# Attention and two gated layers on one core: other planner durations, six planning passes, shorter masks, and a choice of engine for divisions and copies

## Chip, core and metric

One core of one Trainium2 chip runs the whole program. The time is the device time of one execution in microseconds (us); of the kernel before there are three timed runs and one profiled execution. Engine names as in the profile: PE is TensorE, with PEld its weight loads; DVE is VectorE; ACT is ScalarE; POOL is GpSimd; SP is SyncE, which issues nearly all DMAs.

## What is computed

Three stages follow each other; all inputs and outputs are float32 and the weights are given as 64-bit floats (the kernel rebuilds float32 from their two halves).

```python
# 1. attention: 2 batches, 8 heads, 768 positions, head width 64
keep = (pos_k < n_global) | ((rel >= 0) & (rel < n_local))       # 8 and 96
scores = q @ k.T / 8 - slope[h] * dist, -1e9 where not keep
x = softmax(scores) @ v                                          # to (2, 768, 512)
# 2. first gated layer, causal convolution over 5 positions
x = (sigmoid(conv5(x)) * (x @ w_val)) @ w_out
# 3. second gated layer, centred convolution over 3 positions, width 1024
h = relu(x @ w_in)
out = (h * sigmoid(conv3(h))) @ w_out2
```

## The kernel before

**Attention.** Since a query sees the first 32 positions at most and a short band behind itself, there are 12 tiles (2 batches of 6) of 128 queries against at most 256 keys. For each tile and half (4 heads): scores on PE into PSUM (L430); on DVE the masked score and its minimum, by one custom instruction per head that reads the scores from PSUM and the mask `B` from SBUF (L441, "the minimum" below); on ACT the exponential with its sum (L446); on POOL the guard of four sums (L457); on DVE the reciprocal (L460) and one division of the 128x256 (first tile of a batch: 128x128) probabilities per head (L467). PE turns the probabilities, two heads at a time, into PSUM (L491), ACT copies them out (`pts`, L495), PE multiplies by the values (L509), and ACT copies the tile's output into `x` (L526).

**Weights.** A weight of 512 KB is loaded into `raw`, and ACT (L238), POOL (L240) and DVE (twice, L245 and L248) make it float32. There are three `raw` buffers and 24 such loads. The first layer's output weight and the second's input weight are multiplied on PE beforehand (L295, product `W`).

**Gated layers.** They run over four chunks (two per batch, 400 and 368 positions). Matmuls take three products of split halves: a high part made on ACT (L210) and a low part on DVE (L212). `values` makes `gg` from `gx` (L674), `hidden` makes `h` from `gg` and `W` (L715), `gated` makes `g` (L734), `project` the output (PE into bank `s`, copied by L769 and L771). A convolution is one scaled copy for its first tap (L616 on ACT, or L617 on POOL) and DVE multiply-adds for the others (L621).

**What sets the order.** Every step is added to a `Plan` with an engine, an assumed duration and what it reads and writes. `Plan.lay` runs a list schedule backward for ranks and once forward; the order of starts is then the program's order on PE, DVE, ACT and POOL, and within one engine nothing overtakes. Steps with several "ways" go to the engine where the schedule ends them first. Buffers are rings: a step that opens a buffer waits for the users of the one it replaces. Masks are prepared before the plan by hand: distances and their comparisons on DVE, one scaled copy of the mask per head on POOL (L335).

Of the kernel before, what the change touches and what calls it, by code (L numbers as in the profile page):

```python
# [81 lines left out]
class Plan:  # L82
# [31 lines left out]

    def link(self):
# [13 lines left out]
    def lay(self, pred, succ, rank, back):  # L129
# [3 lines left out]
        free = dict.fromkeys(self.LAG, 0.0)  # L133
        mode, est, at = None, dict.fromkeys(self.work, 0.0), {}
# [41 lines left out]
    def issue(self, laid):  # L176
        self.link()
        order = list(self.work)
        if laid:
            back = self.lay(lambda w: w.succ, lambda w: w.pred, lambda w: 0.0, True)  # L180
            for w in self.work:
                w.rank = -back[w] - w.cost + w.bias
            at = self.lay(lambda w: w.pred, lambda w: w.succ, lambda w: w.rank, False)
            order.sort(key=lambda w: at[w])
# [43 lines left out]
def to_f32(c, dst, raw, n, bufs, reads, token):  # L228
# [9 lines left out]
    pl.add("ACT", act_us(n), lambda: nc.scalar.activation(dst(), whole(), AF.Copy, scale=2.0**-112), bufs, reads, [token])  # L238
# [11 lines left out]
    pl.add("DVE", dve_us(n, 0.12), last_bits, bufs, [], [tail])  # L250
    pl.add("DVE", dve_us(n, 0.12), join, bufs, [tail], [token])


def conv_weights(c):
# [3 lines left out]
    c.plan.add("SP", 0.5, lambda: nc.sync.dma_start(raw.rearrange("p d t -> p (d t)"), c.conv_w), writes=["cwr"], delay=2.5)  # L258
# [5 lines left out]
def unit(c, dst, src, a, col, bufs, token, e=None):  # L264
# [3 lines left out]
    c.plan.add("SP", 0.5, dma, [raw], [], [("raw", raw)], delay=4.0)  # L268
# [4 lines left out]
def weights(c):  # L273
# [14 lines left out]
    def product(half):  # L288
        wi = "inb" if half else "ina"
        for cb in range(4):  # L290
            ps = c.ring["f"].new()
            cs, fs = slice(cb * P, (cb + 1) * P), slice(half * 512, (half + 1) * 512)
            for e in range(4):
# [7 lines left out]
                512, [ps], [("wps", half, cb)], ("W", half, cb),  # L301
# [24 lines left out]
def scratch(c):  # L326

    x = [c.x[:, d, XP:] for d in range(NC1)]
    c.rel, c.ge, c.loc, c.d = (x[d][:, 0:WIN] for d in range(4))
    c.key, c.k0, c.d0, ic = (x[d][:, 4 * P : 5 * P] for d in range(4))  # L330
    return c.d.bitcast(I32), ic.bitcast(I32)


def mask_head(c, out, d, h):
    c.nc.gpsimd.tensor_scalar(out, d, -slope(h) / QKSCALE, 1.0, ALU.mult, ALU.mult)  # L335


def first_mask(c):
# [5 lines left out]
    rel, loc, key, k0, d0 = c.rel, c.loc, c.key, c.k0, c.d0  # L344
# [5 lines left out]
    c.b0 = c.const.tile([P, 2, P], F32, name="b0")  # L350
    c.B0 = [c.b0[:, h, :] for h in range(2)]
    for h in range(2):
        mask_head(c, c.B0[h], d0, h)


def masks(c, ap):

    nc, pl = c.nc, c.plan
    ng, nl, rel, loc, d, key = c.ng, c.nl, c.rel, c.loc, c.d, c.key
    c.B = ap.tile([P, NH, WIN], F32, name="B")  # L360
    b0 = ap.tile([P, NH - 2, P], F32, name="b02")
    c.B0 += [b0[:, h, :] for h in range(NH - 2)]
    for h in range(2, NH):
        pl.add("POOL", 0.33, lambda h=h: mask_head(c, c.B0[h], c.d0, h), [], ["d0"], [("B0", h)])

    def distance():
        nc.vector.tensor_scalar(key[:, 0:GW], key[:, 0:GW], ng, None, ALU.is_lt)
        nc.vector.tensor_scalar(d, loc, -BIG, BIG, ALU.mult, ALU.add)
        nc.vector.tensor_scalar(d[:, 0:GW], key[:, 0:GW], -BIG, BIG, ALU.mult, ALU.add)
        nc.vector.tensor_tensor(d[:, GW:], d[:, GW:], rel[:, GW:], ALU.add)  # L370
        nc.vector.tensor_scalar(d[:, 0:GW], d[:, 0:GW], nl, None, ALU.add)
# [583 lines left out]
```

## Time and profile before

| what | us |
|---|---|
| timed runs | 297.34, 297.78 (median), 299.58 |
| profiled execution, its own time | 296.97 |
| its span | 295.2 |
| outside the span | 1.8 |

The span is what the profile shows, and the execution's own time adds 1.8 us around it. Busy time is the time in which an engine works on at least one instruction; on DVE, ACT and PE the end of one record overlaps the start of the next, so the distance from start to start is a little less than a record's length.

### The profile page before, as it was taken

The page shows a single profiled execution, that of the slowest core. Times are in us where ns is not written, and L with a number is a line of the kernel's source. Part 1 is how long each engine was busy: PE and PEld are TensorE (multiplying, and loading weights), DVE is VectorE, ACT ScalarE, POOL GpSimd, SP SyncE. Part 2 cuts the span into 40 slices and gives each one's busy share as a digit, 9 for nine tenths or more (in the row PEclk, how much of TensorE's full clock was granted, in tenths as well). Part 3 has the DMA queues.
Part 4 walks back from the last instruction along what each step waited for, and adds up shares of the span by engine and source line. Part 5 has one row for each costly group of instructions (what it writes and reads, how often), then busy time and mean ns, then how long its engine had stood idle before and what let it go on. Part 6 is the DMA issues. An engine that isn't in the chain of part 4 may idle for free.

```text
span 295.2 us, 5444 instructions
## 1 busy us (share of the span) xinstructions
PE 271.7 (92%) x1832; PEld 227.5 (77%) x1832; DVE 238.3 (81%) x638; ACT 198.8 (67%) x498; POOL 57.4 (19%) x153
## 2 busy tenths in 40 slices
PE   2398897999998999999999999999999999999990
PEld 2366775664554699999898899989999988999890
DVE  4789998899999999999799999999996643367500
ACT  2589999998386879798689663895466523466410
POOL 2831112234211210032212440011220200000000
PEclk9999999999999999999999999999999999999998
DMA  4953478564514521002412000000000000000111
GB/s 139 361 221 112 149 255 273 180 194 163 165 52 142 154 107 38 19 2 95 151 49 71 2 1 36 3 0 36 36 2 37 36 2 36 36 2 3 71 73 44
DMA packets 10277, 26.18 MB, mean 89 GB/s; under 512 B 1408, under 2 KB 2688, under 8 KB 10240
## 3 DMA queue, kind: packets, MB, share of 16 engines
q1 hardware_dynamic: 9440, 25.22, 25.1%
q10 hardware_dynamic: 800, 0.52, 0.6%
q8 instruction: 16, 0.26, 0.4%
q14 instruction: 21, 0.17, 0.2%
HBM read 22.59 MB, written 3.15 MB: 87 GB/s over the span
## 4 chain that ended last, share of the span: by engine, by line
PE 75%; DMA 8%; ACT 5%; issue 4%; DVE 3%; SPq 2%; POOL 1%; POOLq 0%; DVEq 0%; ACTq 0%
PE f L295 8%; PE f L219 8%; PE s L220 7%; PE s L221 7%; PE s L219 7%; PE f L221 7%; PE f L220 7%; PE x L509 4%; PE t L491 3%; PE s L430 3%; ACT p L446 3%; DMA v<-in_v_dram 3%; PE x L221 2%; PE t L221 2%; PE x L219 2%
## 5 line engine op out<-in xcount | busy, mean ns | idle before, releaser
L446 ACT ACTIVATE p<-p,st 128x256 f32<-128x256 f32 (+1 forms) x96 | 46.0, 483 | 7.8 <-DVE st L441 7.7
L621 DVE SCALAR_TENSOR_TENSOR z<-h,cw,z 128x384 f32<-128x384 f32 x64 | 39.9, 633 | 8.5 <-ACT z L616 7.1
L220 PE MATMUL s<-w,g 128*128 128x512 f32 (+1 forms) x104 | 39.5, 379 | 0.0
L221 PE MATMUL s<-w,g 128*128 128x512 f32 (+1 forms) x104 | 39.2, 377 | 0.0
L219 PE MATMUL s<-w,g 128*128 128x512 f32 (+1 forms) x104 | 39.1, 376 | 0.0
L623 ACT ACTIVATE z<-z 128x384 f32<-128x384 f32 (+2 forms) x48 | 25.0, 523 | 18.8 <-DVE z L621 18.8
L491 PE MATMUL t<-ident,p 128*128 128x128 f32 x176 | 29.0, 284 | 8.9 <-DVE p L467 4.8
L621 DVE SCALAR_TENSOR_TENSOR z<-x,cw,z 128x400 f32<-128x400 f32 (+1 forms) x64 | 36.9, 616 | 0.0
L491 PEld LDWEIGHTS t<-ident,p 128*128 128x128 f32 x176 | 20.2, 142 | 20.5 <-ACT pts L495 8.5
L441 DVE CUSTOM_DVE_ANT_0 p<-s,B 128x256 f32<-128x256 f32 x80 | 30.9, 414 | 3.7 <-POOL kq L474 1.4
L467 DVE TENSOR_SCALAR p<-p,st 128x256 f32<-128x256 f32 (+1 forms) x96 | 31.8, 369 | 0.4
L295 PE MATMUL f<-w,w 128*128 128x512 f32 x64 | 30.8, 604 | 0.0
L495 ACT ACTIVATE pts<-t 128x512 f32<-128x512 f32 (+1 forms) x48 | 26.5, 551 | 5.6 <-PE t L491 3.6
L219 PE MATMUL f<-gg,Wh 128*128 128x400 f32 (+1 forms) x80 | 27.7, 347 | 0.0
L221 PE MATMUL f<-gg,Wl 128*128 128x400 f32 (+1 forms) x80 | 27.1, 338 | 0.0
L220 PE MATMUL f<-gg,Wh 128*128 128x400 f32 (+1 forms) x80 | 27.0, 338 | 0.0
L212 DVE TENSOR_TENSOR g<-z,g 128x384 fp32r<-128x384 f32 x32 | 17.4, 551 | 9.9 <-ACT g L210 9.9
L430 PE MATMUL s<-kq 64*128 64x128 f32 x320 | 24.1, 289 | 0.5 <-POOL kq L474 0.5
L430 PEld LDWEIGHTS s<-kq 64*128 64x128 f32 x320 | 20.3, 193 | 4.7 <-issue 2.7
L509 PE MATMUL x<-pts,v 128*64 128x128 f32 x320 | 22.1, 278 | 2.0 <-ACT x L526 1.2
L240 POOL TENSOR_SCALAR raw<-raw 128x512 f32<-128x512 f32 x24 | 18.1, 757 | 28.9 <-ACT m L238 19.3
L734 DVE SCALAR_TENSOR_TENSOR z<-z,h 128x384 f32<-128x384 f32 x32 | 18.0, 565 | 5.7 <-ACT z L623 5.6
(117 smaller groups left out, 595.2 us busy)
## 6 DMA issues: line engine op xcount, KB each, us to landing
raw<-in_moe_w_out_dram SPq DMA_DIRECT2D x12, 512.0 KB, 3.5
kq<-in_kq_dram SPq DMA_DIRECT2D x11, 512.0 KB, 4.7
raw<-in_moe_w_in_dram SPq DMA_DIRECT2D x8, 512.0 KB, 4.0
v<-in_v_dram SPq DMA_DIRECT2D x11, 256.0 KB, 4.5
out_dram<-o SPq DMA_DIRECT2D x11, 256.0 KB, 2.0
raw<-in_moe_w_val_dram SPq DMA_DIRECT2D x4, 512.0 KB, 3.4
v<-in_v_dram SPq DMA_DIRECT2D x8, 64.0 KB, 2.7
x<-in_kq_dram ACTq DMA_DIRECT2D x1, 256.0 KB, 4.1
```

Source lines behind the costliest of these rows:

```text
L219: nc.tensor.matmul(out, lh, rh, start=first, stop=False)
L220: nc.tensor.matmul(out, lh, rl, start=False, stop=False)
L221: nc.tensor.matmul(out, ll, rh, start=False, stop=last)
L295: nc.tensor.matmul(ps.t, big["wot"].t.bitcast(F32)[:, e, cs], big[wi].t.bitcast(F32)[:, e, :], start=e == 0, stop=e == 3)
L430: nc.tensor.matmul(out, keys(t0, pr, 1)[hs], keys(j, pr, 0)[hs], start=True, stop=True)
L441: nc.vector.tensor_tensor_reduce(w.t[:, :nk], sc, bias, -QKSCALE, 3.0e38, ALU.add, ALU.min, st.t[:, 0, h : h + 1])
L446: nc.scalar.activation(w.t[:, :nk], w.t[:, :nk], AF.Exp, bias=st.t[:, 0, h : h + 1], scale=-1.0, accum_out=st.t[:, 1, h : h + 1],)
L467: nc.vector.tensor_scalar(w.t[:, :nk], w.t[:, :nk], st.t[:, 2, h : h + 1], None, ALU.mult)
L491: nc.tensor.transpose(o[:, z, n, :], p[2 * pr + z].t[:, n * P : (n + 1) * P], ident)
L495: nc.scalar.activation(w.t[:, :, :nw, :], o[:, :, :nw, :], AF.Copy)
L509: nc.tensor.matmul(o[z * D : (z + 1) * D, pr, :], vals(j, 2 * pr + z), pts[pr].t[:, z, n, :], start=n == 0, stop=n == len(js) - 1,)
L621: nc.vector.scalar_tensor_tensor(z(), src(k), w()[:, k : k + 1], z(), ALU.mult, ALU.add)
```

## The change

The planner gets other assumed durations (formulas for ACT, DVE and POOL, loads by their bytes, other start offsets), a price for leaving a kind of matmul on PE (`STICK`), and six backward and forward passes of which the best is kept. The masks are made by fewer operations, with positions written as float32 directly. Four kinds of step get a second or third engine: the scaled mask copies (POOL, ACT or DVE), the division (DVE or POOL), the copy of the turned probabilities and the copy of a tile's output (ACT or DVE). The first tap had two engines before; its split changes through the durations.

```diff
+LANDING = 2.4
@@ class Plan
+    START = {"DVE": 0.4, "ACT": 1.2, "SP": 0.3}
+    STICK = 3.0
+    PASSES = 6
@@ lay
+        free.update({} if back else self.START)
-                    w = min((w for w in ws if est[w] <= t), key=rank)
+                    w = min((w for w in ws if est[w] <= t), key=lambda w: rank(w) + (self.STICK if not back and e == "PE" and w.mode != mode else 0.0))
@@ issue
-            back = self.lay(lambda w: w.succ, lambda w: w.pred, lambda w: 0.0, True)
...
+            for _ in range(self.PASSES):
+                back = self.lay(lambda w: w.succ, lambda w: w.pred, lambda w: -after[w], True)
...
+                if best is None or end < best[0]:
+                    best = end, at, {w: w.eng for w in order}
@@ durations
-def act_us(n, psum=False, sums=False):
-    return 0.115 + 0.000714 * n + 0.09 * sums
-def dve_us(n, extra=0.07):
-    return extra + 0.00104 * n
+def act_us(n, sbuf=True, scaled=False, sums=False):
+    return 0.05 + 0.000834 * n + 0.042 * sbuf + 0.092 * scaled + 0.093 * sums
+def dve_us(n, scaled=False):
+    return 0.069 + 0.001042 * n + 0.061 * scaled
-    return 0.12 + 0.0018 * n
+    return 0.17 + 0.0013 * n
+def dma_us(kb):
+    return max(0.4, kb / 385.0)
@@ masks
-    nc.vector.scalar_tensor_tensor(loc, rel, nl, c.ge, ALU.is_lt, ALU.mult)
-    nc.vector.scalar_tensor_tensor(d0, rel[:, P:], nl, loc[:, P:], ALU.subtract, ALU.mult)
-    nc.vector.scalar_tensor_tensor(k0, key, ng, loc[:, P:], ALU.is_lt, ALU.max)
-    nc.vector.tensor_scalar(k0, k0, -BIG, BIG, ALU.mult, ALU.add)
-    nc.vector.scalar_tensor_tensor(d0, d0, nl, k0, ALU.add, ALU.add)
+    nc.vector.tensor_scalar(c.far, c.key, ng, BIG, ALU.is_ge, ALU.mult)
+    nc.vector.scalar_tensor_tensor(w, rel, nl, c.far, ALU.is_ge, ALU.mult)
+    nc.vector.scalar_tensor_tensor(c.d0, rel, nl, w, ALU.min, ALU.add)
...
+def head_ways(c, n, out, d, h):
+    nc, k = c.nc, -slope(h) / QKSCALE
+    return {
+        "POOL": (0.02 + pool_us(n), lambda: nc.gpsimd.tensor_scalar(out(), d, k, 1.0, ALU.mult, ALU.mult)),
+        "ACT": (act_us(n), lambda: nc.scalar.activation(out(), d, AF.Copy, scale=k)),
+        "DVE": (0.07 + 0.00052 * n, lambda: nc.vector.tensor_scalar(out(), d, k, None, ALU.mult)),
+    }
@@ division
+                def on_pool(h=h, st=st, w=p[h], nk=nk):
+                    nc.gpsimd.tensor_scalar(w.t[:, :nk], w.t[:, :nk], st.t[:, 2, h : h + 1], 1.0, ALU.mult, ALU.mult)
+                pl.add(
+                    "DVE", 0.13 + 0.00052 * nk, on_dve, [p[h], st], [("r", t, half)], [("p", t, h)],
+                    POOL=(0.1 + pool_us(nk), on_pool),
+                )
@@ copy of the turned probabilities; the copy of a tile's output likewise
+                "ACT", act_us(2 * nk, False), copy, [pt, pts[pr]], [("pt", t, pr)], [("pts", t, pr)],
+                DVE=(dve_us(2 * nk), by_dve),
@@ before the plan
-        nc.vector.tensor_copy(c.rel, it)
-        nc.vector.tensor_scalar(c.ge, c.rel, 0.0, None, ALU.is_ge)
-        nc.vector.tensor_copy(c.key, ic)
```

Counted over the whole order, these steps change engine: 50 of 96 divisions go from DVE to POOL (42 of 256 columns, 8 of 128); 16 of 48 copies of turned probabilities (10 of 512 columns, 6 of 256) and 3 of 12 copies into `x` go from ACT to DVE; 9 of 16 scaled mask copies leave POOL, 7 for DVE and 2 for ACT; 13 first taps go from ACT to POOL. PE has the same 1832 matmuls; the number of stretches of one kind of matmul falls from 118 to 113.

On PE, at the start of the plan, tile 0's scores are `s<-x`, tile 1's are those that read `kq`, and `t<-ident,p` turns tile 0's probabilities. Before:

```order
L430 MATMUL s<-x 128x128 x8
L491 MATMUL t<-ident,p 128x128 x2
L430 MATMUL s<-x,kq 128x128 x2
L430 MATMUL s<-kq 128x128 x2
L430 MATMUL s<-x,kq 128x128 x2
L430 MATMUL s<-kq 128x128 x2
L491 MATMUL t<-ident,p 128x128 x2
L430 MATMUL s<-x,kq 128x128 x2
```

And now:

```order
L461 MATMUL s<-x 128x128 x8
L461 MATMUL s<-x,kq 128x128 x2
L461 MATMUL s<-kq 128x128 x2
L461 MATMUL s<-x,kq 128x128 x2
L461 MATMUL s<-kq 128x128 x2
L461 MATMUL s<-x,kq 128x128 x2
L461 MATMUL s<-kq 128x128 x2
L461 MATMUL s<-x,kq 128x128 x2
L461 MATMUL s<-kq 128x128 x2
L528 MATMUL t<-ident,p 128x128 x4
```

Tile 1's scores stood behind the turning of tile 0 and stand directly behind tile 0's scores now.

On DVE, from the read of the two mask bounds (`lf`) to the first minimum (printed as ISA `p,st`; `x` holds the masks' scratch, the last row of the three branch rows ends the part ahead of the plan). Before:

```order
L342 CAST lf<-li 128x2
L345 SCALAR_TENSOR_TENSOR x<-x,lf 128x256
L346 SCALAR_TENSOR_TENSOR x<-x,lf 128x128
L347 SCALAR_TENSOR_TENSOR x<-x,lf 128x128
L348 TENSOR_SCALAR x<-x 128x128
L349 SCALAR_TENSOR_TENSOR x<-x,lf 128x128
L911 ISA
L911 REGISTER_ALU x3
L911 COMPARE_AND_BRANCH
L367 TENSOR_SCALAR x<-x,lf 128x32
```

And now:

```order
L371 CAST lf<-li 128x2
L374 TENSOR_SCALAR x<-x,lf 128x128
L375 SCALAR_TENSOR_TENSOR x<-x,lf 128x128
L376 SCALAR_TENSOR_TENSOR x<-x,lf 128x128
L957 ISA
L957 REGISTER_ALU x3
L957 COMPARE_AND_BRANCH
L385 TENSOR_SCALAR b_224<-x 128x128 x3
L472 ISA p,st<-s,b_224 128x128
```

Three operations ahead of `lf` (two casts and a comparison) are gone as well, three of its five followers remain in smaller form, and three mask copies stand ahead of the first minimum, while the distance of the 256 wide mask has moved behind the fifth.

On POOL, around the second batch's second and third tile (`st` is the guard, `raw` a weight, `p` a division, `kq<-gl` puts the global keys into a tile's keys). Before:

```order
L474 TENSOR_SCALAR kq<-gl 128x4x32
L240 TENSOR_SCALAR raw<-raw 128x512 x2
L457 TENSOR_SCALAR st<-st 128x4
L240 TENSOR_SCALAR raw<-raw 128x512 x2
L474 TENSOR_SCALAR kq<-gl 128x4x32
```

And now:

```order
L488 TENSOR_SCALAR st<-st 128x4
L264 TENSOR_SCALAR raw<-raw 128x512
L501 TENSOR_SCALAR p<-p,st 128x256 x4
L264 TENSOR_SCALAR raw<-raw 128x512 x2
L488 TENSOR_SCALAR st<-st 128x4
L501 TENSOR_SCALAR p<-p,st 128x256 x4
L511 TENSOR_SCALAR kq<-gl 128x4x32
```

Up to four divisions in a row stand between two guards, and the conversion of weights stands among them.

## Rows read from the trace of the kernel before

**Rows 1.** The page: busy time of PE, DVE, ACT, POOL with share and instructions.
```profile
PE 271.7 (92%) x1832; PEld 227.5 (77%) x1832; DVE 238.3 (81%) x638; ACT 198.8 (67%) x498; POOL 57.4 (19%) x153
```

**Rows 2.** Windows of 15 us: length, then busy time (and instructions) by engine, clock, DMA.
```profile
15.00:30.00 15.00, 13.00 (x151) 10.34 (x152) 12.98 (x62) 14.35 (x50) 3.84 (x11) 1.00 0.45 158
30.00:45.00 15.00, 13.64 (x166) 10.72 (x162) 14.35 (x57) 13.88 (x43) 2.59 (x8) 1.00 0.63 204
45.00:60.00 15.00, 13.51 (x126) 9.36 (x126) 12.91 (x50) 14.67 (x48) 3.74 (x8) 1.00 0.65 217
60.00:75.00 15.00, 14.94 (x81) 7.90 (x78) 14.91 (x48) 11.97 (x36) 4.91 (x9) 1.00 0.52 175
...
225.00:240.00 15.00, 15.00 (x82) 13.98 (x81) 9.08 (x17) 7.79 (x16) 2.45 (x17) 1.00 0.09 36
```

**Rows 3.** Timeline at the start of hidden's second chunk: start, length, engine, what.
```profile
156.66 0.99 DVE L212 TENSOR_TENSOR gg<-z,gg 128x368 fp32r<-128x368 f32 x2 [0.23 <-ACT gg L210]
157.61 0.40 PE L221 MATMUL s<-w,g 128*128 128x512 f32 x1
157.85 0.33 PE L219 MATMUL f<-gg,Wh 128*128 128x368 f32 x1
```

**Rows 4.** Timeline of the first 18 us, pieces of DVE and of SP's queue.
```profile
4.75 0.16 DVE L342 CAST lf<-li 128x2 f32<-128x2 int32 x1
...
5.41 0.34 SPq L403 DMA_DIRECT2D kq<-in_kq_dram  x1
...
7.11 0.24 DVE L367 TENSOR_SCALAR x<-x,lf 128x32 f32<-128x32 f32 x1 [0.38 <-issue]
...
14.60 0.42 DVE L441 CUSTOM_DVE_ANT_0 p<-s,B 128x256 f32<-128x256 f32 x1 [1.03 <-PE s L430]
...
17.45 0.42 DVE L441 CUSTOM_DVE_ANT_0 p<-s,B 128x256 f32<-128x256 f32 x1 [1.39 <-POOL kq L474]
```

**Rows 5.** The page's DMA issues: count, KB of each, median us from issue to landing.
```profile
kq<-in_kq_dram SPq DMA_DIRECT2D x11, 512.0 KB, 4.7
...
li<-in_n_dram SPq DMA_DIRECT2D x1, 2.0 KB, 3.4
```

**Rows 6.** Groups of equal shape: count, busy us, mean ns of one, idle before.
```profile
L467 DVE TENSOR_SCALAR p<-p,st 128x256 f32<-128x256 f32 x80 | 26.2, 364 | 0.4
L212 DVE TENSOR_TENSOR Wl<-f,Wh 128x512 fp32r<-128x512 f32 x8 | 5.4, 679 | 0.0
L335 POOL TENSOR_SCALAR B<-x 128x256 f32<-128x256 f32 x8 | 3.2, 410 | 0.5
L240 POOL TENSOR_SCALAR raw<-raw 128x512 f32<-128x512 f32 x24 | 18.1, 757 | 28.9 <-ACT m L238 19.3 <-ACT w L238 9.6
```

**Rows 7.** Timeline: divisions on DVE alone, beside mask copies and beside a conversion on POOL.
```profile
11.66 0.47 DVE L467 TENSOR_SCALAR p<-p,st 128x128 f32<-128x128 f32 x2
12.26 0.77 POOL L335 TENSOR_SCALAR B<-x 128x256 f32<-128x256 f32 x2
12.43 1.14 DVE L467 TENSOR_SCALAR p<-p,st 128x128 f32<-128x128 f32 x4
...
56.88 0.93 DVE L467 TENSOR_SCALAR p<-p,st 128x128 f32<-128x128 f32 x2
56.94 0.79 POOL L240 TENSOR_SCALAR raw<-raw 128x512 f32<-128x512 f32 x1 [0.37 <-ACT w L238]
```

**Rows 8.** The chain that ended last, its end: start, us, what.
```profile
285.06 0.61 ACT o L769
...
285.68 4.02 DMA out_dram<-o
...
289.92 0.42 DVE o L771
```

**Rows 9.** The same chain in its middle, one stretch of scores and one of turning.
```profile
65.46 1.09 PE s L430 x16
...
72.98 0.44 PE t L491 x4
```

More of the change, by code (lines that the diff above doesn't have):

```diff
@@ L113, in add, with any @@
         return w
+    def any(self, ways, bufs=(), reads=(), writes=()):
+        e = next(iter(ways))
+        us, fn = ways.pop(e)
+        return self.add(e, us, fn, bufs, reads, writes, **ways)
     def link(self):
@@ L179, in issue @@
         if laid:
-            back = self.lay(lambda w: w.succ, lambda w: w.pred, lambda w: 0.0, True)
[L181 to L184, printed above, removed]
+            after, best = dict.fromkeys(order, 0.0), None
+            for _ in range(self.PASSES):
+                back = self.lay(lambda w: w.succ, lambda w: w.pred, lambda w: -after[w], True)
+                for w in order:
+                    w.rank = -back[w] - w.cost + w.bias
+                at = self.lay(lambda w: w.pred, lambda w: w.succ, lambda w: w.rank, False)
+                after = {w: at[w] + w.cost for w in order}
+                end = max(after.values())
+                if best is None or end < best[0]:
+                    best = end, at, {w: w.eng for w in order}
+            end, self.at, engs = best
+            for w in order:
+                w.eng = engs[w]
+                w.cost = w.ways[w.eng][0]
+            order.sort(key=lambda w: self.at[w])
         for w in order:
@@ L237, in to_f32 @@
     tail = (token, "tail")
-    pl.add("ACT", act_us(n), lambda: nc.scalar.activation(dst(), whole(), AF.Copy, scale=2.0**-112), bufs, reads, [token])
+    pl.add("ACT", act_us(n) + 0.05, lambda: nc.scalar.activation(dst(), whole(), AF.Copy, scale=2.0**-112), bufs, reads, [token])
     pl.add(
@@ L267, in unit @@
     dma = lambda: nc.sync.dma_start(raw.t.rearrange("p d t -> p (d t)"), rows(src, a, col))
-    c.plan.add("SP", 0.5, dma, [raw], [], [("raw", raw)], delay=4.0)
+    c.plan.add("SP", dma_us(512), dma, [raw], [], [("raw", raw)], delay=LANDING)
     view = (lambda: raw.t) if e is None else (lambda: raw.t.rearrange("p (e x) t -> p e x t", e=e))
@@ L328, in scratch, with positions @@
     x = [c.x[:, d, XP:] for d in range(NC1)]
[L329 to L335, printed above, removed]
+    c.rel, c.w, c.d = (x[d][:, 0:WIN] for d in range(3))
+    c.key, c.far, c.d0 = (x[d][:, 4 * P : 5 * P] for d in range(3))
+def positions(c):
+    nc = c.nc
+    nc.gpsimd.iota(c.rel, pattern=[[-1, WIN]], base=P, channel_multiplier=1, allow_small_or_imprecise_dtypes=True)
+    nc.gpsimd.iota(c.key, pattern=[[1, P]], base=0, channel_multiplier=0, allow_small_or_imprecise_dtypes=True)
+    nc.gpsimd.affine_select(
+        out=c.rel, in_=c.rel, compare_op=ALU.is_ge, fill=BIG, base=P, pattern=[[-1, WIN]], channel_multiplier=1
+    )
 def first_mask(c):
@@ L351, in first_mask @@
-    c.B0 = [c.b0[:, h, :] for h in range(2)]
-    for h in range(2):
-        mask_head(c, c.B0[h], d0, h)
+    rel, w = c.rel[:, P:], c.w[:, P:]
+    nc.vector.tensor_scalar(c.far, c.key, ng, BIG, ALU.is_ge, ALU.mult)
[8 more added lines that the diff above has]
+    }
@@ L356, in masks @@
 def masks(c, ap):
     nc, pl = c.nc, c.plan
-    ng, nl, rel, loc, d, key = c.ng, c.nl, c.rel, c.loc, c.d, c.key
+    ng, nl, rel, w, d = c.ng, c.nl, c.rel, c.w, c.d
     c.B = ap.tile([P, NH, WIN], F32, name="B")
[L361 to L364, printed above, removed]
+    b0 = ap.tile([P, NH, P], F32, name="b0")
+    c.B0 = [b0[:, h, :] for h in range(NH)]
@@ L366, in distance @@
+    for h in range(NH):
+        pl.any(head_ways(c, P, lambda h=h: c.B0[h], c.d0, h), [], ["d0"], [("B0", h)])
     def distance():
[L367 to L371, printed above, removed]
@@ L373, in masks @@
-    pl.add("DVE", 1.1, distance, [], [], ["d"])
+        nc.vector.tensor_scalar(w[:, GW:], rel[:, GW:], nl, BIG, ALU.is_ge, ALU.mult)
+        nc.vector.scalar_tensor_tensor(d[:, GW:], rel[:, GW:], nl, w[:, GW:], ALU.min, ALU.add)
+        nc.vector.tensor_scalar(d[:, 0:GW], c.far[:, 0:GW], nl, None, ALU.add)
+    pl.add("DVE", 0.75, distance, [], [], ["d"])
     for h in range(NH):
-        pl.add("POOL", 0.6, lambda h=h: mask_head(c, c.B[:, h, :], d, h), [], ["d"], [("B", h)])
+        pl.any(head_ways(c, WIN, lambda h=h: c.B[:, h, :], d, h), [], ["d"], [("B", h)])
@@ L529, in fast_attention @@
             [xp], [("xp", t, pr) for pr in range(NPAIR)], [("x", i)] + (["d", "d0"] if t in (0, 1, 4) else []),
+            DVE=(
+                dve_us(512),
+                lambda xp=xp, i=i: nc.vector.tensor_copy(
+                    c.x[:, :, XP + i * P : XP + (i + 1) * P], xp.t.rearrange("p (a q) -> p a q", q=P)
+                ),
+            ),
         )
@@ L621, in tap @@
             nc.vector.scalar_tensor_tensor(z(), src(k), w()[:, k : k + 1], z(), ALU.mult, ALU.add)
-        pl.add("DVE", dve_us(n, 0.13), tap, bufs, reads, [token])
+        pl.add("DVE", dve_us(n, True), tap, bufs, reads, [token])
     pl.add("ACT", act_us(n), lambda: nc.scalar.activation(z(), z(), AF.Tanh, scale=0.5), bufs, [], [token])
@@ L771, in copy @@
                 nc.vector.tensor_scalar(o.t[:, :w], po[n].t[:, :w], 0.5, None, ALU.mult)
-        pl.add("ACT" if n < nt else "DVE", act_us(w), copy, [po[n], o], [("po", b, ch, n)], [("o", b, ch, n)])
+        pl.add("ACT" if n < nt else "DVE", act_us(w, False), copy, [po[n], o], [("po", b, ch, n)], [("o", b, ch, n)])
         t1 = ch * CH + t * P
         pl.add(
-            "SP", 0.5, lambda o=o, t1=t1, c0=c0, w=w: nc.sync.dma_start(c.out[b, t1 : t1 + P, c0 : c0 + w], o.t[:, :w]),
-            [o], [("o", b, ch, n)], [], delay=2.0,
+            "SP", dma_us(w // 2), lambda o=o, t1=t1, c0=c0, w=w: nc.sync.dma_start(c.out[b, t1 : t1 + P, c0 : c0 + w], o.t[:, :w]),
+            [o], [("o", b, ch, n)], [], delay=LANDING,
         )
@@ L806, in attention_gated_mlps @@
         nc.scalar.dma_start(v0, v[0, 0:P].rearrange("s (a h) d -> s a h d", a=4))
[L807 to L809 removed]
+        scratch(c)
+        positions(c)
         nc.vector.memset(one, 0.0)
```

49 lines of the change are left out of this document (24 added, 25 removed).

## The prediction

> **What bounds the kernel now.** I read the page's busy times first. PE works in 92% of the span, DVE in 81%, ACT in 67%, POOL in 19% [rows 1]. That says PE, but the share is an average over stages, so the windows come next. From 15 to 60 us, while attention runs and weights are made, PE has idle time in each window, and DVE and ACT are nearly full: DVE 12.98, 14.35 and 12.91 of 15, ACT 14.35, 13.88 and 14.67 [rows 2]. From 60 us on PE is full; a window at 225 shows it at 15.00 while DVE has fallen to 9.08 [rows 2]. So PE can't do more late, and what is to be won lies ahead of 60 us, in work that starves there for DVE and ACT.
>
> It is not enough that PE is full, though. Its order is fixed, and it stops where DVE is late. The place where this nearly happens is the start of the second chunk of `hidden`, its 97th matmul from `gg`. The low half of the last `gg` that it needs is done at 156.66 + 0.99 = 157.65, and the matmul starts at 157.85, one matmul's distance (0.24) behind the one at 157.61 [rows 3]. DVE arrives just in time there. I therefore count how much earlier or later DVE gets to this point, and PE's end moves with it: the sum is over DVE's work in front of it, plus what PE has left behind it.
>
> **The change part by part.** All is counted against the profiled execution, 296.97 us (295.2 of span and 1.8 around it), which is 0.8 under the median of the timed runs.
>
> Masks. From `lf` to the plan's first DVE operation go 7.11 - 4.75 = 2.36 us with five operations and a branch of 0.38 [rows 4]. `lf` itself needs the two bounds, issued at 0.74 and landed 3.4 later, at 4.1 [rows 5]; what stood before it on DVE is gone. With `lf` at 4.15, 0.2 for it, three operations at about 0.36 (five in 2.36 - 0.16 - 0.38) and the branch, the plan starts on DVE at 5.8 instead of 7.11: -1.3. The mask copies that DVE takes over are in its load below.
>
> Tile 1's scores no longer stand behind the turning of tile 0. DVE waited 1.03 for them at 14.60 and 1.39 more before their second half at 17.45 [rows 4]. The keys, issued at 5.41 [rows 4] with 4.7 to landing [rows 5], are there at about 10, so both waits can go: -2.4. If the cover is another wait at the same place, 0.
>
> Later waits. DVE's idle time from 15 to 60 is 2.02 + 0.65 + 2.09 = 4.8; without the 1.39 it is 3.4 [rows 2, 4]. ACT is the fuller engine in two of the three windows, and over the whole run ACT gives up 16 copies of turned probabilities, 3 output copies and 13 first taps, some 14 us by lengths near 0.5. DVE then waits less for it. But POOL's guard, behind which the reciprocal waits, now stands among divisions. Bounds 0 and -3.4; I take two thirds, -2.3.
>
> DVE's own load in front of the point. 42 divisions of 256 columns leave. A record is 0.36 [rows 6], and start to start 0.10 less, 0.26; eight of 128 columns count 0.20: -12.6. Copies out of PSUM come: the nearest DVE operation is the low half `Wl` of 512 columns, 0.679 [rows 6], so 0.60 from start to start and 0.34 for 256 columns. Ten and six copies, and three into `x`: 6.0 + 2.0 + 1.8 = +9.8. Seven mask copies at 0.14 to 0.20 less the shorter distance: +1.0. The order also puts two more weight conversions with one split in front and one gating step behind: 5 x 0.60 - 0.94 = +2.1. Sum +0.3: what the divisions free, the copies and the reordering fill.
>
> The shared cost of DVE and POOL. Two divisions of 128 columns alone take 0.47 [rows 7], so four take about 0.87. Four beside two mask copies on POOL take 1.14 [rows 7]: 0.27 late. Two beside a conversion on POOL take 0.93 instead of 0.47 [rows 7]: 0.46 late within its 0.79. So POOL's work holds DVE up, and moving a division to POOL doesn't free DVE of all of it. No trace shows a division on POOL; the nearest row is the mask copy, the same operation with a constant, 0.410 for 256 columns [rows 6], so I take 0.45. Upper bound: every one meets a DVE operation as the conversion did, 0.46 / 0.79 = 0.58 of its length, 0.26. Lower bound: nothing, beside the minima, which read one operand from PSUM. By the nearest row, the eight 256-column mask copies cost about 0.5 in all (the 0.27 and a similar one before it), 0.06 each. 42 x 0.06 + 8 x 0.04 = 2.8; four first taps on POOL ahead of the point, longer, at 0.17 each 0.7; mask copies that leave POOL -0.3. I take +3.2; the ends are +0 and +13.5.
>
> The Trainium skill, SBUF — State Buffer, section Who interferes with whom, says that a DVE instruction in a 2-port mode or with two SBUF inputs and a GpSimd instruction that reads SBUF exclude each other for the whole instruction, and that a DVE instruction with at most one SBUF input is not held up. [rows 7] agree for the divisions. By that rule nearly every moved division would block DVE for its length where such an operation is next, which is the slower rival below; with 0.45 in each of 50 places the sum would end above 310.
>
> PE. Of the output's matmuls 12 instead of 15 stand in front of the point, so 3 x 0.24 = +0.7 is left behind it. 113 instead of 118 stretches: nothing to half a microsecond, taken as nothing.
>
> The end. The last copy on DVE waits for an output buffer: the copy at 285.06, its DMA 4.02, then 289.92 [rows 8]. In the new order 33 instead of 27 matmuls of 256 columns follow the one that this copy needs, at 0.12 (half of 0.24): the wait ends 0.7 earlier against PE's end, -0.7.
>
> SP's loads of the output weight move a few places forward and the key loads of the second batch back; the three `raw` buffers still let one in only when DVE is done with another, so I give this nothing.
>
> Sum: -1.3 - 2.4 - 2.3 + 0.3 + 3.2 + 0.7 - 0.7 = -2.5, 296.97 - 2.5 = 294.5 us.
>
> **The rivals.** First, faster: the point at 157.85 doesn't bind and the first chunk's matmuls from `gg` set the time. In front of these DVE has 3.9 less (44 divisions 11.0, 8 minima 2.7 and two reciprocals 0.3 fewer; copies 5.6, masks 1.0 and seven multiply-adds 3.6 more). With -1.3 - 2.4 - 2.3 and four fifths of the shared cost, +2.6, DVE is there 7.3 earlier. PE has one stretch of scores (1.09) and two of turning (0.44 each) less in front [rows 9], so 2.0 more behind: -5.3, with the end -6.0, 291.0 us. For it speaks PE's idle time up to 60; against it that DVE gets to both points with the same operations, and has none to spare between them.
>
> Second, slower: the shared cost is the upper one. The three or four divisions in a row on POOL meet conversions and divisions on DVE each time, and the guard behind them comes late. With +13.5 the sum is +7.8, 304.8 us. It decides from the price of one division: at 0.11 the sum is zero, from 0.19 the kernel is more than 1% slower. For it speaks the 0.93 beside the conversion; against it the mask copies, the nearest row, with 0.06.
>
> Third, the gain doesn't come: the early waits turn into other waits (the exponential's chain, landings) and what is left cancels, 297.0 us. For it speaks that DVE's load is the same to 0.3; against it the mask part, which nothing hides.
>
> **How the numbers follow.** The forecast has 0.40, the faster rival 0.26, the slower 0.17, no change 0.17. About 1%, 3 us, is what a measurement of this kernel can tell from no change; from the median of 297.78 that is below 294.8 or above 300.8. The forecast lies at the lower edge, so about half of it counts as faster: 0.40 x 0.55 + 0.26 = 0.48. Within: 0.40 x 0.43 + 0.17 x 0.9 = 0.33. The rest, 0.19, is slower. The range goes from the faster rival without shared cost, 291.0 - 2.6 = 288.4, to a price of 0.2 for a division, 301.5: 288.5 to 301.5.
>
> **What would show it.** Right: the first minimum some 1.3 to 2 us earlier; tile 1's minima without the two waits; records of L498 and of the weight conversions stretched beside L501 on POOL, some 3 us in all; ACT with idle time between 15 and 60; the second chunk's first matmul from `gg` again right behind its last low half, near 156. Wrong: that matmul starts well behind DVE (then PE or ACT binds), or L501 stretches DVE by 0.15 or more each, or DVE shows new idle time ahead of the reciprocals.

## The result and the profile after

The changed kernel takes 289.06 us (median of 288.42 to 289.27) where the kernel before took 297.70 beside it: ratio 0.9694, interval 0.9651 to 0.9737, 8.6 us less. The profiled execution has 289.12 instead of 296.97 (-7.85), its span 286.9 instead of 295.2 (-8.3), and 2.2 instead of 1.8 lie outside the span. The direction was forecast, the size was not: -2.5 had been expected. Executions of one kernel can differ by some 3 us with the granted clock of PE (last section), so "at like clock" below sets only those above 0.990 side by side, and one execution each of e5 and e13, more than 1.5% above the fastest of its kernel, is left out of medians and ratios.

The page of the changed kernel, busy times and the chain's shares by engine (before: [rows 1]).

```profile
PE 270.1 (94%) x1832; PEld 227.9 (79%) x1832; DVE 238.6 (83%) x607; ACT 187.2 (65%) x468; POOL 95.4 (33%) x208
...
PE 73%; DVE 15%; POOL 3%; issue 3%; ACT 3%; POOLq 1%; DVEq 0%; ACTq 0%
```

DVE's busy time is the same to 0.3 us, ACT's is 11.6 less, POOL's 38 more. The windows of the changed kernel, the same cuts as [rows 2] and then three longer ones:

```profile
15.00:30.00 15.00, 13.45 (x151) 10.36 (x148) 14.90 (x61) 13.80 (x46) 8.40 (x19) 1.00 0.69 229
30.00:45.00 15.00, 13.49 (x131) 9.66 (x132) 14.90 (x49) 12.58 (x38) 7.99 (x16) 1.00 0.64 206
45.00:60.00 15.00, 15.00 (x109) 9.22 (x110) 14.82 (x51) 13.23 (x38) 8.60 (x14) 1.00 0.63 220
...
0.00:60.00 60.00, 49.46 (x449) 35.90 (x450) 53.99 (x207) 48.00 (x149) 32.48 (x74) 1.00 0.67 225
60.00:105.00 45.00, 43.63 (x310) 30.16 (x308) 44.07 (x113) 33.43 (x90) 20.19 (x30) 1.00 0.39 125
105.00:150.00 45.00, 45.00 (x390) 41.58 (x387) 43.92 (x112) 33.79 (x88) 21.92 (x46) 1.00 0.26 82
```

The three longer windows in the kernel before:

```profile
0.00:60.00 60.00, 45.34 (x472) 34.60 (x474) 48.77 (x208) 48.63 (x158) 17.89 (x54) 1.00 0.62 208
60.00:105.00 45.00, 43.29 (x275) 25.25 (x272) 44.74 (x124) 31.99 (x82) 11.89 (x20) 1.00 0.47 153
105.00:150.00 45.00, 45.00 (x370) 42.06 (x369) 42.15 (x119) 38.32 (x99) 8.68 (x26) 1.00 0.19 65
```

Half of the gain lies ahead of 60 us: PE has 4.1 us more busy time there, DVE 5.2. DVE has almost no idle time left from 15 to 60 (0.4 instead of 4.8). From 60 to 150 PE gains only 0.3 more, and 2.3 us come at the very end (e7 below).

Of PE's 4.1 us, 2.3 lie even ahead of 15 us (7.52 instead of 5.19 busy). Behind its first scores PE stood still until tile 0's first divisions were done; now tile 1's scores come first. Timeline of the kernel before, then of the changed one:

```profile
11.89 0.66 PE L491 MATMUL t<-ident,p 128*128 128x128 f32 x2 [4.84 <-DVE p L467]
```

```profile
9.04 0.80 PE L461 MATMUL s<-x,kq 64*128 64x128 f32 x4 [2.08 <-DVE st L472]
```

Something else stands out on PE: the product of the two weights (`f<-w,w`), 64 long matmuls, begins 10 us earlier. Timeline of the kernel before and of the changed one, first rows of the product:

```profile
47.50 1.02 PE L295 MATMUL f<-w,w 128*128 128x512 f32 x2
```

```profile
37.83 1.12 PE L319 MATMUL f<-w,w 128*128 128x512 f32 x2
```

At the prediction's point, the second chunk of `hidden`, the changed kernel's timeline reads (before: [rows 3]):

```profile
151.34 0.40 PE L245 MATMUL s<-w,g 128*128 128x512 f32 x1
...
151.57 0.33 PE L243 MATMUL f<-gg,Wh 128*128 128x368 f32 x1
...
152.52 0.53 DVE L236 TENSOR_TENSOR gg<-z,gg 128x368 fp32r<-128x368 f32 x1
...
153.24 0.33 PE L244 MATMUL f<-gg,Wh 128*128 128x368 f32 x1
```

PE arrives 6.3 us earlier (157.85 to 151.57), DVE only 4.6 (157.65 to 153.05), and yet PE doesn't wait. In the kernel before, DVE made the four low halves in the order 2, 1, 3, 0, so the second matmul needed the last one. Now it makes them in the order 0, 1, 2, 3, and the last one is first read by the eleventh matmul, at 153.24.

### The profile page after: what moved, and what is told of

Same layout as the page of the kernel before. It is cut to its first block, busy times and chain, and to the rows that moved or that the text cites. A ratio compares the mean times of both kernels' runs of the same rounds, so it can differ in the third digit from the quotient of the medians.

```text
span 286.9 us, 5416 instructions
## 1 busy us (share of the span) xinstructions
PE 270.1 (94%) x1832; PEld 227.9 (79%) x1832; DVE 238.6 (83%) x607; ACT 187.2 (65%) x468; POOL 95.4 (33%) x208
## 4 chain that ended last, share of the span: by engine, by line
PE 73%; DVE 15%; POOL 3%; issue 3%; ACT 3%; POOLq 1%; DVEq 0%; ACTq 0%
PE s L244 8%; PE s L245 8%; PE s L243 8%; PE f L243 7%; PE f L245 7%; PE f L244 7%; PE s L461 4%; PE x L553 4%; PE t L528 4%; DVE p L472 3%; DVE z L671 2%; PE t L243 2%; PE t L245 2%; PE x L245 2%; PE x L244 2%
## 5 line engine op out<-in xcount | busy, mean ns | idle before, releaser
L671 DVE SCALAR_TENSOR_TENSOR z<-x,cw,z 128x400 f32<-128x400 f32 (+1 forms) x64 | 39.6, 643 | 0.2
L501 POOL TENSOR_SCALAR p<-p,st 128x256 f32<-128x256 f32 (+1 forms) x50 | 32.5, 660 | 11.0 <-DVE st L491 8.7
L472 DVE CUSTOM_DVE_ANT_0 p<-s,B 128x256 f32<-128x256 f32 x80 | 30.5, 410 | 0.0
L461 PE MATMUL s<-kq 64*128 64x128 f32 x320 | 25.7, 292 | 0.8 <-DVE st L472 0.7
L461 PEld LDWEIGHTS s<-kq 64*128 64x128 f32 x320 | 21.5, 194 | 4.9 <-issue 2.6
L667 POOL TENSOR_SCALAR z<-h,cw 128x384 f32<-128x384 f32 x10 | 8.9, 887 | 45.9 <-DVE z L671 31.0
L245 PEld LDWEIGHTS s<-w,g 128*128 128x128 f32 x104 | 19.5, 188 | 3.8
L244 PEld LDWEIGHTS s<-w,g 128*128 128x128 f32 x104 | 19.6, 188 | 2.8
```

The costliest lines, as they stand in the source:

```text
L244: nc.tensor.matmul(out, lh, rl, start=False, stop=False)
L245: nc.tensor.matmul(out, ll, rh, start=False, stop=last)
L461: nc.tensor.matmul(out, keys(t0, pr, 1)[hs], keys(j, pr, 0)[hs], start=True, stop=True)
L472: nc.vector.tensor_tensor_reduce(w.t[:, :nk], sc, bias, -QKSCALE, 3.0e38, ALU.add, ALU.min, st.t[:, 0, h : h + 1])
L501: nc.gpsimd.tensor_scalar(w.t[:, :nk], w.t[:, :nk], st.t[:, 2, h : h + 1], 1.0, ALU.mult, ALU.mult)
L671: nc.vector.scalar_tensor_tensor(z(), src(k), w()[:, k : k + 1], z(), ALU.mult, ALU.add)
```

## The experiments

Theory A: the engine choices and masks make the gain. Theory B: the planner's order makes it. The first four runs take the change apart.

```diff
# e1: the kernel before with the planner's part only (START, STICK, PASSES, LANDING, the new durations)
# e2: the kernel before with the new ways and masks only (old durations, one pass); from its edit:
+                    POOL=(0.1 + pool_us(nk), on_pool),
+                DVE=(dve_us(2 * nk), by_dve),
+def head_ways(c, n, out, d, h):
...
# e3: the changed kernel without
-                    POOL=(0.1 + pool_us(nk), on_pool),
# e4: the changed kernel with first_mask, masks and scratch of before
```

> The kernel before with the planner's part alone: the new durations, START, STICK, six passes; masks and engines as before. Theory A (the engines make the gain: work leaves DVE and ACT between 15 and 60 us, and PE starves less there): 295.5 to 297.5, PE's lost time up to 60 us within 1 of before. Theory B (the order makes the gain: the weight product starts some 10 us earlier because the planner now knows what loads and conversions cost): 290 to 292.5, the first matmul of the product near 38 instead of 47.5. The sum of the prediction gives this part its tile 1 term and half of the later waits, with two conversions more in front: 295 to 297.

> The kernel before with the new engine choices and the shorter masks, planned by the old durations in one pass (47 divisions go to POOL, 6 copies of turned probabilities and 1 output copy to DVE). Theory A: most of the gain is here, 289.5 to 292. Theory B: 295 to 297. If the two parts only work together, both this kernel and the planner's part alone stay above 294.

> The changed kernel with all 96 divisions on DVE, planned anew (7 copies of turned probabilities stay on DVE, none of the output copies). If a division on POOL costs DVE about 0.1 (5 us in all) against 13 us that it frees, DVE is the fuller by some 8 less the 5 us of copies that go back to ACT: 291 to 293. If the shared cost eats the gain, 288 to 289.5.

> The changed kernel with the mask making of before (three operations more ahead of the read of the bounds, five instead of three behind it, all scaled copies on POOL), planned anew. If the early start is carried to the end one to one: 290.4 (the 1.3 of the prediction) to 291.5 (with the start of the first matmuls). If the early time is taken up by PE's later work: 289.1 as the changed kernel, within 0.5.

The kernel before took 297.5 to 298.2 in all comparisons; the changed one is set beside them with its 289.06.

| run | us | beside |
|---|---|---|
| e1 planner only | 292.11 | before 297.47: -5.4, 0.9796 (0.9729 to 0.9863) |
| e2 engines and masks only | 295.63 | -1.8, 0.9895 (0.9819 to 0.9971) |
| e3 all divisions on DVE | 290.75 | changed 289.06: +1.7 |
| e4 old masks | 291.43 | +2.4 |

Theory B holds for the larger part: masks, divisions and copies are untouched in e1 (only 15 first taps move from ACT to POOL), and it has 5.4 of the 8.6. By the timeline of e1 the product starts at 36.76, and its windows show DVE 2.7 and PE 1.5 fuller ahead of 60 than before:

```profile
0.00:60.00 60.00, 46.80 (x428) 33.89 (x430) 51.49 (x197) 46.03 (x141) 27.00 (x60) 1.00 0.69 228
```

Two things are hidden in these 5.4. First, part of them is the end: in e1 the last output copy no longer waits for a buffer (e7 below has what that is worth), while in e2 it still waits for a store, as before (it starts at 289.46, the last matmul at 287.42). Timeline of e1, its last copy, behind a last matmul at 284.30:

```profile
284.67 0.42 DVE L811 TENSOR_SCALAR o<-s 128x256 f32<-128x256 f32 x1 [8.82 <-PE s L245]
```

Second, e1 gains nothing ahead of 15 us, where PE still waits 5.05 for tile 0's first divisions; its 1.5 comes from 15 to 60.

Engines and masks bring 1.8 under the old order (e2) and 3 on top of the new one. But two of e2's four executions lost clock (0.990 and 0.988); the two others, 293.88 and 294.84, are 2.9 below the kernel before at like clock. So the two parts about add up, and it isn't shown that they need each other. (Under the old durations e2 makes other choices: 47 divisions go to POOL, only 7 copies to DVE.)

In e3 PE is as full up to 60 as in the changed kernel (49.63), but then waits once, 1.6 us, which is about its loss. It is not at the prediction's point (154.3 there) but ahead of it, in `values`. There PE needs a bank that ACT empties, and ACT's copy stands behind conversions of `gg` that had waited for DVE. A window and the timeline of e3:

```profile
105.00:150.00 45.00, 43.39 (x385) 40.32 (x384) 44.17 (x116) 34.03 (x86) 12.18 (x30) 1.00 0.22 70
```

```profile
147.26 0.91 ACT L234 ACTIVATE gg<-z 128x368 fp32r<-128x368 f32 x2 [0.36 <-DVE z L723]
...
148.08 0.58 ACT L569 ACTIVATE x<-x 128x512 f32<-128x512 f32 x1
...
148.72 0.43 PE L243 MATMUL x<-gx,wvh 128*128 128x368 f32 x1 [1.61 <-ACT x L569]
```

The next four ask whether it is the earlier weights as such, what the passes do, and what the end costs.

```diff
# e5, the changed kernel
-    PASSES = 6
+    PASSES = 1
# e6, the kernel before; e8, the changed kernel
-EARLY = -5.0
+EARLY = -20.0
# e7, the kernel before: the last output copy gets a tile of its own
+        if n == nt:
+            o.own = c.own_o
...
```

> The changed kernel planned in one pass instead of six; durations, engines and masks as changed. In its order the weight product stands behind six tiles of scores and a half, close to before, where the changed kernel has it behind five. Theory B (the order of the weights makes most of the gain): 292.5 to 295, first matmul of the product at 43 or later, PE's lost time up to 60 us 24 or more instead of 21.6. Theory A (engines and masks make it, with the durations): 289 to 290.5.

> The kernel before with one number changed: the bias EARLY, by which the planner prefers the weights, from -5 to -20. In its order the first matmul of the weight product stands behind four tiles of scores instead of nearly six. Theory B: 291.5 to 294 with no new engine, mask or duration, the product's first matmul before 42 and PE's lost time up to 60 us 2 to 5 less than the 28.1 of before. If earlier weights only push attention back and PE waits for that later: 296.5 to 298.

> The kernel before, its order untouched, where the last output copy on DVE has a buffer of its own instead of the one that waits for a store. If that wait stands in the end's way by its whole length, the copy starts 0.3 behind the last matmul instead of at 289.92, some 1.8 earlier: 295.5 to 296.2. If the last store then queues behind the one before it and lands no earlier: 297.4.

> The changed kernel with EARLY at -20 instead of -5: the product's first matmuls stand behind four and a half tiles of scores instead of five, the later ones too. If PE's idle time before 60 us is still what can be won by order: 286.5 to 288.5. If the tiles that are put back make PE wait at the end of attention: 289 to 292.

(PE's lost time of 28.1 and 21.6 in these texts is not the idle time of the windows, which is 14.7 and 10.5 up to 60 us.)

e5: 292.53 (291.59 to 294.20), ratio 0.9814 (0.9739 to 0.9889), 3.5 more than the changed kernel: one pass loses some two fifths of the gain. e6 was a miss for theory B in its simple form: 303.23 against 298.20, ratio 1.0153 (1.0081 to 1.0225), slower although the product starts at 40.1. Attention falls behind there (48 minima done by 60 us instead of 56), DVE's busy time up to 60 is 47.61 (less than before), and PE stands still in three places, each followed by a lower clock (last section). The clock is the larger share: of the 6.8 us that its span is longer, 4.5 are PE's busy time for the same matmuls (276.2 instead of 271.7), as three stretches of some 3.4 us at half the clock would make 5 (estimate), and 2.3 are idle time. e8: 290.53, 1.5 more. So earlier weights are not good as such. My reading is that an order counts in which DVE doesn't stand still and PE has the product's matmuls to fill its waits; no run isolates this, and which of the planner's durations carries it, beside the passes, wasn't tried.

e7 shows the end. Timeline of the kernel before, then of e7, then of the changed kernel, last matmul and last copy:

```profile
287.76 0.28 PE L221 MATMUL s<-w,g 128*128 128x256 f32 x1
...
289.92 0.42 DVE L771 TENSOR_SCALAR o<-s 128x256 f32<-128x256 f32 x1 [9.63 <-DMA out_dram<-o]
```

```profile
288.42 0.28 PE L221 MATMUL s<-w,g 128*128 128x256 f32 x1
...
288.73 0.43 DVE L773 TENSOR_SCALAR o<-s 128x256 f32<-128x256 f32 x1 [7.77 <-PE s L221]
```

```profile
281.78 0.28 PE L245 MATMUL s<-w,g 128*128 128x256 f32 x1
...
282.15 0.42 DVE L821 TENSOR_SCALAR o<-s 128x256 f32<-128x256 f32 x1 [8.82 <-PE s L245]
```

From the last matmul to the end of the span it is 7.4 in the kernel before, 5.1 in e7 (293.5) and 5.1 in the changed kernel. e7 takes 296.01, ratio 0.9933 (0.9891 to 0.9976); at like clock it is 1.2 less (297.21 beside it). The wait for the store is gone in both.

Four more test the prediction's premise and ACT, and try a better number.

```diff
# e9 the kernel before, e10 the changed kernel
+        for _ in range(4 if writes == ("gg", 0, 1, 3) else 1):
             nc.vector.tensor_tensor(lo(), src(), hi().bitcast(F32), ALU.subtract)
...
# e11, the changed kernel
-                DVE=(dve_us(2 * nk), by_dve),
# (the way of the output copy likewise)
# e12, the changed kernel
-                    "DVE", 0.13 + 0.00052 * nk, on_dve, ...
+                    "DVE", 0.2 + 0.00052 * nk, on_dve, ...
```

> The kernel before, its order untouched, with the low half of the last gg of the second chunk written four times instead of once, so that DVE reaches the point of the prediction (157.65) three operations of 0.46, some 1.4 us, later. The prediction's premise (PE's end moves with DVE's arrival there): 298.2 to 298.6, by 1.2 to 1.4 more. Theory C (PE does not wait there: the first matmul needs only the first of four gg, and the low half of the last is read ten matmuls of 0.16, 1.6 us, after the start at 157.85; PE is full since 105 and what it lost earlier sets the end): 0 to 0.4 more.

> The same three operations more in the changed kernel, where the matmuls of that chunk start at 151.6 and the low half is done at 153.0, ten matmuls or 1.6 us behind the start being 153.2. Theory C with a start that DVE now just meets: 1.0 to 1.4 more than the changed kernel's 289.1. If PE has slack there too: 0 to 0.4 more.

> The changed kernel with the copies of turned probabilities and of outputs on ACT alone, planned anew (38 divisions on POOL). If ACT is what holds DVE and PE up between 15 and 60 us (the prediction's later waits): 290.5 to 293, with DVE idle there again by 1.5 or more. If DVE's own load binds, which loses some 7 us of copies and takes back 3 us of divisions: 287 to 289.

> The changed kernel with the planner's duration of a division on DVE raised by 0.07 to 0.33 for 256 columns, nearer to what it takes beside POOL's divisions (records of 0.47 on the mean in the changed kernel, 0.36 before). 54 divisions go to POOL instead of 50, and the weight product stands half a tile of scores earlier. If the planner's numbers are what counts: 287 to 288.8. If the order it finds is as good by chance: within 1.5 of 289.1 on either side.

e9: 299.46 against 297.75, +1.7 (ratio 1.0051, 1.0014 to 1.0087); e10: 291.27, +2.2. Theory C, that PE doesn't wait there, falls: a late DVE counts in both. (1.4 us were added on DVE; PE's own waits there are 1.25 and 1.39, and the rest is within the spread of the executions.) The timeline of e9:

```profile
158.79 0.33 PE L224 MATMUL f<-gg,Wh 128*128 128x368 f32 x1
160.36 0.19 PEld L225 LDWEIGHTS f<-gg,Wh 128*128 128x128 f32 x1 [1.62 <-DVE gg L213]
```

It is the second matmul that waits, as the order of the low halves says; the text of e9 had put the read ten matmuls behind the start. e11: 290.05, 1.0 more, although DVE's idle time up to 60 is 3.4 longer again (busy 50.56 instead of 53.99): by taking 19 copies from ACT, DVE is filled with work that it would else have had time for. PE is as full there as in the changed kernel (49.24), so DVE's idle time is not by itself what sets the time. e12: 287.39 (286.95 to 290.56), ratio 0.9679 (0.9609 to 0.9750): 1.7 below the changed kernel by the medians, with intervals that overlap. A truer duration may be worth as much as a whole engine choice; four executions don't show it.

The last four ask what set the end before: DVE at the point, or PE by itself.

```diff
# e13, e15: second chunk of hidden
-            for d in range(NC1):
+            for m, d in enumerate((2, 1, 3, 0) if (b, ch) == (0, 1) else range(NC1)):
...
# e14, e15: first chunk of hidden; leaves out 9 of its 96 matmuls (384 are those of all four chunks)
+                if (b, ch) == (0, 0) and f < 3 and d == 1:
+                    continue
# e16: conversion of the first weight
+        for _ in range(4 if token == ("ina", 0) else 1):
             nc.vector.scalar_tensor_tensor(high(), low(), 29, high(), ...)
```

> The kernel before, order of the steps untouched, where the second chunk's matmuls read the four gg in the order 2, 1, 3, 0 in which DVE finishes their low halves (before: 0 to 3, so the second matmul waits for the last). That eases DVE's side of the point by nine matmuls of 0.16, 1.5 us, and leaves PE's. If DVE's arrival alone sets the end: 1.2 to 1.5 less than before. If PE arrives at the same time by its own work (two gates): within 0.4 of before.

> The kernel before without 9 of the 384 matmuls of hidden's first chunk (one of four gg for three of eight outputs, so what follows is computed from incomplete sums): PE's side of the point eased by 9 x 0.17 = 1.5 us, DVE's not. If DVE's arrival binds as well (two gates): 0.2 to 0.6 less, and the second matmul from gg waits about 1.1 for DVE. If PE's own time alone sets the end: 1.3 to 1.6 less.

> Both edits, order 2, 1, 3, 0 and 9 matmuls fewer (again with incomplete sums). Two gates: 1.3 to 1.6 less than before, more than the sum of the two alone. One gate: no more than the better of the two alone.

> The kernel before, order untouched, with one DVE operation of the first weight's conversion (near 19 us) done four times instead of once: 3 x 0.6 = 1.8 us more on DVE ahead of a stretch where it has 4.8 us of idle time up to 60. If DVE work counts in full wherever it stands in front of the point, as in the prediction's sum: 1.5 to 2.0 more. If the idle time behind it takes it up: 0 to 0.8 more.

| run | us (before 297.69) | ratio and interval |
|---|---|---|
| e13 DVE's side eased | 297.81 | 0.9999 (0.9965 to 1.0033) |
| e14 PE's side eased by 1.5 | 296.09 | 0.9952 (0.9918 to 0.9985) |
| e15 both | 296.32 | 0.9954 (0.9910 to 0.9998) |
| e16 1.8 more on DVE at 19 us | 300.08 | 1.0050 (1.0014 to 1.0085) |

Easing DVE's side gives nothing, easing PE's gives its 1.5 in full, and both give no more. So before the change PE's own time set the end, within intervals of about 1 us. With two gates PE would have waited 1.1 for DVE in e14. Its timeline shows why it doesn't:

```profile
155.38 0.99 DVE L212 TENSOR_TENSOR gg<-z,gg 128x368 fp32r<-128x368 f32 x2 [0.23 <-ACT gg L210]
...
156.17 0.33 PE L219 MATMUL f<-gg,Wh 128*128 128x368 f32 x1
156.42 0.19 PEld L220 LDWEIGHTS f<-gg,Wh 128*128 128x128 f32 x1 [0.30 <-DVE gg L212]
```

DVE came 1.3 earlier as well (156.37 instead of 157.65), with no work taken from it. What it does there follows PE's `values`: its 2.85 us of idle time from 105 to 150 were waits, and they shrink when PE is earlier. In e16 the 1.8 us count in full (+2.4, and +2.0 at like clock): the idle time up to 60 doesn't take them up. That it is itself waiting on the same chain is likely, not shown. DVE's work early in the program does move the end, then, though at the point PE leads.

## Why the prediction was wrong in size

The step that failed is the premise "I therefore count how much earlier or later DVE gets to this point, and PE's end moves with it". It holds in one direction only. A later DVE moves the end (e9, e10), an earlier one by itself does not (e13); what moves it is PE's own lost time ahead (e14), and most of that lies before 60 us, where the sum had no term for PE. PE reaches the point 6.3 us earlier: 4.4 of this is idle time that is gone (4.1 before 60 us, 0.3 after), 0.7 by the prediction's count are the three output matmuls that now stand behind the point, and the other 1.2 aren't accounted for. The other orders roughly fit this: PE's idle time up to 150 us is 16.4 in the kernel before, 14.3 in e1, 14.2 in e3, 13.2 in e8, 12.9 in e11, 11.9 in the changed kernel and 11.7 in e12, with spans of 295.2, 290.7, 289.0, 287.8, 288.4, 286.9 and 285.4. The planner hides this: by its durations it fills PE with output matmuls up to the moment at which DVE is due, so the two can meet at that point whichever of them leads, and the meeting proves nothing. By its own terms:

- Masks, -1.3: right. DVE's first operation of the plan starts at 5.93 instead of 7.11, the first minimum at 6.57 instead of 8.27. Undoing the masks costs 2.4, though (e4); its order was planned anew as well, so whether an early start is worth more than its length stays open.
- Tile 1, -2.4: right, less a new wait. Timeline of the changed kernel's start:

```profile
5.93 0.72 DVE L385 TENSOR_SCALAR b<-x 128x128 f32<-128x128 f32 x3 [0.45 <-DVE x L376]
6.57 0.28 DVE L472 CUSTOM_DVE_ANT_0 p<-s,b 128x128 f32<-128x128 f32 x1
...
11.12 0.42 DVE L472 CUSTOM_DVE_ANT_0 p<-s,B 128x256 f32<-128x256 f32 x1
...
13.29 0.42 DVE L538 COPY pts<-t 128x256 f32<-128x256 f32 x1 [0.85 <-PE t L528]
```

The waits of 1.03 and 1.39 [rows 4] are gone; a copy waits 0.85 for PE instead.
- Later waits, -2.3: too small, and the cause was wrong. Up to 60 us DVE lost 5.2 of its idle time against the 4.7 of both terms, and 1.1 more from 60 to 150, where I had counted none. I had put this down to ACT's lighter load. But the first taps couldn't help there: ACT's first one starts at 68.2 in the kernel before. And e1, where no copy leaves ACT, gains 2.7 of the 5.2, while e11, with the copies back on ACT, loses only 1.0 of time. About half came with the order alone (e1).
- DVE's load and the shared cost, +0.3 and +3.2: nearly right. DVE arrives 4.6 earlier with 6.3 less idle time, so it does 1.7 more in front of the point; with the masks' 1.3 I had 2.2. The shared cost by itself: what DVE's records exceed the lower quartile of their line and shape (those by over 0.04 counted) comes to 8.3 in e3 and 12.9 in the changed kernel, so 4.6 for 50 divisions, 0.09 each, between two kernels of different order. I had 0.06, and at 0.11 the sum would have been zero. The length of a division on POOL was mis-sized too: 0.70 for 256 columns, where 0.45 was taken. The groups of the changed kernel (before: [rows 6]):

```profile
L501 POOL TENSOR_SCALAR p<-p,st 128x256 f32<-128x256 f32 x42 | 28.8, 696 | 10.7 <-DVE st L491 8.7 <-PE f L244 0.8 <-PE f L245 0.7
...
L498 DVE TENSOR_SCALAR p<-p,st 128x256 f32<-128x256 f32 x38 | 16.9, 470 | 0.0
...
L538 DVE COPY pts<-t 128x512 f32<-128x512 f32 x10 | 6.8, 679 | 0.0
...
L236 DVE TENSOR_TENSOR Wl<-f,Wh 128x512 fp32r<-128x512 f32 x8 | 5.3, 675 | 0.0
```

The copy's 0.679 is what the low half of 512 columns had stood in for. A division left on DVE takes 0.47 instead of 0.36.
- PE: 0.7 left behind the point was expected; its start is 6.3 earlier and its last matmul 6.0, so 0.3. Not foreseen was that PE may now start 1.5 ahead of the end of DVE's last low half. The order of the four halves allows it, and the prediction has no term for which matmul reads which.
- The end, -0.7: mis-sized. I had only moved the wait along with the matmuls behind it; it went altogether, -2.3 (7.4 to 5.1).

Sum as measured: DVE's arrival -4.6, PE's start ahead of it -1.7, behind the point +0.3, the end -2.3, together -8.3 of span. Beside the forecast, DVE's arrival is 2.1 off (-2.5 from the first five terms), PE's start ahead of it 1.7 (no term), the part behind the point 0.4 and the end 1.6.

The faster rival (291.0) was the nearer one, for a reason that it gave: PE's idle time up to 60. That the point doesn't bind, its condition, is what e13 shows of the kernel before; that DVE sets the time at the first chunk instead is not so, since its last low half there is done at 117.01 and PE's first matmul from `gg` starts at 118.70. It expected DVE 7.3 earlier at the first chunk; that chunk's first matmul starts 8.8 earlier (118.7 to 109.9). The slower rival failed on its price. The Trainium skill, SBUF — State Buffer, section Who interferes with whom, which the prediction set beside it, is borne out in kind: in the rows below the minima (L472, one operand from PSUM) keep 0.41 beside a division on POOL, while divisions on DVE stretch. But the exclusion for a whole instruction, at 0.45 in 50 places, is not what it came to; the measured 0.09 decides. Timeline of the changed kernel:

```profile
48.28 0.59 POOL L501 TENSOR_SCALAR p<-p,st 128x256 f32<-128x256 f32 x1
48.44 0.41 DVE L472 CUSTOM_DVE_ANT_0 p<-s,B 128x256 f32<-128x256 f32 x1
...
48.78 1.02 DVE L498 TENSOR_SCALAR p<-p,st 128x256 f32<-128x256 f32 x2
48.84 0.82 POOL L264 TENSOR_SCALAR raw<-raw 128x512 f32<-128x512 f32 x1
```

## What to carry to other kernels

Where a planner fits engines to each other, the place at which two of them meet tells nothing about which one leads; count each engine's lost time up to there, and ease each side by itself in a run. A change of assumed durations is a change of the kernel: here it made more than half of the gain with masks, divisions and copies untouched, and one pass instead of six lost some two fifths of it. A mechanism read off a result (the earlier weights) is worth a run of its own before it is believed: forced by one number, it made the kernel slower, mostly by the clock that PE lost behind its waits.

## What the runs showed of the hardware

PE's idle time can cost more than its length. Windows of e2 around 50 us, where PE waits 2.26 us for a late load of `v`, up to 48.98:

```profile
46.00:49.00 3.00, 0.74 (x4) 0.02 (x2) 3.00 (x10) 3.00 (x10) 2.41 (x5) 1.00 0.79 302
49.00:50.00 1.00, 1.00 (x16) 0.83 (x16) 0.58 (x1) 0.65 (x3) 0.02 (x1) 1.00 0.25 74
50.00:51.00 1.00, 1.00 (x8) 0.67 (x6) 0.39 (x4) 0.00 (x1) 0.00 (x0) 0.61 0.91 299
51.00:52.00 1.00, 1.00 (x8) 0.82 (x8) 1.00 (x5) 1.00 (x3) 0.48 (x1) 0.50 0.53 213
52.00:53.00 1.00, 1.00 (x3) 0.50 (x2) 0.88 (x3) 1.00 (x6) 0.00 (x0) 0.50 0.00 0
53.00:54.00 1.00, 1.00 (x5) 0.45 (x4) 0.00 (x0) 0.21 (x1) 0.00 (x0) 0.69 0.10 16
```

PE works 0.74 of 3 us, takes up work again, and from about 50.2 to 53.6 its granted clock is 0.50, the lower of its two levels (1.2 instead of 2.4 GHz). e6 shows this in three places, near 25, 39 and 104 us, and e16 in two, each behind a stretch in which PE stood still for 1.0 to 2.2 us. Not every such stretch does it: in the kernel before PE worked 0.16 of the 5 us from 7 to 12, and its clock stayed at 1.00. Of 31 executions of the kernel before beside e13 to e16, 7 had a mean granted clock of 0.987 to 0.989 and took 299.8 to 300.3; the others lay at 0.992 or more and at 296.7 to 299.2. The changed kernel's four lay within 0.9 us. The two profiled executions that are compared here have a clock of 1.00 in every window shown, so the 8.3 us of span owe nothing to it.
